# Where the first group's square and the weights' rests are computed, in a fused attention and two-stage MLP kernel on one core

## The chip, the core and the metric

The kernel runs on one core of one Trainium2 chip. The metric is the device time of one execution in microseconds (us), and smaller is better. The engines are called PE (matrix multiply), DVE (vector), ACT (scalar, activation), POOL (GpSimd) and SP (which issues most DMAs). PEld is the loading of weights into PE. Each engine takes its own instructions in order, and engines wait for one another by semaphores.

## The reference

Three stages are chained. The change lies in the second, and in what prepares its weights.

```python
# 1. attention with a window of 32, half of the heads dilated by 4 (4 x 8 heads x 576 positions x 64)
attn = softmax(where(mask, q @ k.T / 8, -1e9)); x = attn @ v          # -> x: 2304 x 512
# 2. a dense two-layer block, 512 -> 2048 -> 512
h = x @ w_in
r = maximum(h, 0)
g = s * (r * r) + b                                                   # s, b: one number each
y = g @ w_out
# 3. each token goes to the best of 8 experts (512 -> 1024 -> 512), times its gate
out[token] = gate * (maximum(y @ w1[e], 0) @ w2[e])
```

The weights of stage 2 (`w_in`, `w_out`) arrive as 64-bit floats, so they are converted on the chip.

## The kernel before, in words

**Numbers in two parts.** PE multiplies a rounded 32-bit format (F32R). Each operand X is kept as a rounded part and a rest, X = hi + lo, and `mm3` (L271) issues three matmuls: hi·hi, hi·lo, lo·hi. So whatever enters a matmul is first rounded by one engine (a copy to F32R on ACT), and then its rest is taken as a subtraction.

**Stage 2.** The 2304 tokens go in six groups `g` of 384. For each group the hidden width of 2048 is walked in 16 chunks `fc` of 128. `gemm1(g, fc)` (L277) does 12 matmuls into `ph`, then four elementwise steps on 128 x 384: ACT takes `r` = relu (L284), DVE makes `r` = s·r·r (L285), ACT rounds `gh` = r + b (L288), DVE takes the rest `gl` = (r + b) − gh (L289). `gemm2(g, fc)` (L293) multiplies gh, gl by the chunk's `woh`, `wol` into three accumulators `py`, two chunks behind `gemm1`. The tiles r, gh, gl have two buffers each.

**Weights.** `weight_prep(which, fc)` (L246) converts one tile of 128 x 512. `which` is 0 for `w_in` (tiles `wih`, `wil`) and 1 for `w_out` (tiles `woh`, `wol`). The steps are: SP loads `raw` (L252 or L255, three buffers), DVE shifts (`cv`, L260, two buffers), ACT scales (`ce`, L262, one buffer), POOL adds the two (L263), DVE merges sign and exponent (L264), ACT rounds to `wih` or `woh` (L267), and the rest is taken (L269): on DVE for `w_in`, on POOL for `w_out`. There are 32 such tiles: eight are begun while the first eight units of attention run (`attn_first`, L183), and the others are called two for each turn of the main loop (L356 to L385) during the first group.

**Attention** runs in units. `attn_b` computes scores on PE (`pS`, L128) and the softmax: L134, L137 on DVE, exp L139 on ACT, L141, L142 and the scaling of `prob` (L145) on DVE. `attn_c` transposes `prob` on PE (`pT`, L153) and copies it (`sT`, L158, ACT); `attn_d` multiplies by v on PE (`po`, L172). The units of the next group are put between the chunks of this one at fixed slots. Before the main loop PE also transposes the experts' embedding (`pemb`, L347), whose load `embn` (L344) takes one of the three `raw` buffers.

**Order.** In the main loop PE's instructions stand in the order in which the program is written. The order on DVE, ACT, POOL and SP is made by a planner that simulates the program with costs of its own and starts what it takes to be ready. The experts' stage follows after the last group.

Of the kernel before, what the change touches and what calls it, by code (L numbers as in the profile page):

```python
# [7 lines left out]
F32 = mybir.dt.float32  # L8
# [3 lines left out]
AF = mybir.ActivationFunctionType  # L12
ALU = mybir.AluOpType
# [15 lines left out]
PERIOD, START = 6, 2  # L29
LA = 2  # L30
EARLY = 10
SPLIT = EARLY - LA

P = 128
# [13 lines left out]
class Kern:  # L48
# [180 lines left out]
    def weights_setup(self, left, right):  # L229
        self.xhi, self.xlo, self.wih, self.wil, self.woh, self.wol = [[] for _ in range(6)]  # L230
        for f in range(16):
            pool = right if f < SPLIT else left
            self.woh.append(pool.tile([P, DM], F32R, name=f"woh{f}"))
            self.wol.append(pool.tile([P, DM], F32R, name=f"wol{f}"))
        for f in range(16):
            pool = right if f < EARLY else left
            self.wih.append(pool.tile([P, 4, P], F32R, name=f"wih{f}"))
# [8 lines left out]
    def weight_prep(self, which, fc):  # L246
        nc, sp = self.nc, self.spool
        u = f"{which}{fc}"
        raw = sp.tile([P, 512, 2], I32, tag="raw", name=f"raw{u}", bufs=3)
        fs = slice(P * fc, P * fc + P)  # L250
        if which == 0:
            nc.sync.dma_start(out=raw.rearrange("p f w -> p (f w)"), in_=self.w_in.bitcast(I32)[fs])  # L252
            hi, lo = (x[fc].rearrange("p k f -> p (k f)") for x in (self.wih, self.wil))
        else:
            nc.sync.dma_start(out=raw.rearrange("p f w -> p (f w)"), in_=self.w_out.bitcast(I32)[fs])  # L255
            hi, lo = self.woh[fc], self.wol[fc]
        w0, w1 = raw[:, :, 0], raw[:, :, 1]
        t = sp.tile([P, 512], I32, tag="cv", name=f"cv{u}", bufs=2)
        e = sp.tile([P, 512], I32, tag="ce", name=f"ce{u}", bufs=1)
        nc.vector.tensor_scalar(out=t, in0=w1, scalar1=3, scalar2=0x3FFFFFFF,  # L260
                                op0=ALU.logical_shift_left, op1=ALU.bitwise_and)
        nc.scalar.mul(e, w0.bitcast(U32), 2.0 ** -29)  # L262
        nc.gpsimd.tensor_tensor(out=t, in0=t, in1=e, op=ALU.add)  # L263
        nc.vector.scalar_tensor_tensor(out=t, in0=w1, scalar=-0x40000000, in1=t,  # L264
                                       op0=ALU.bitwise_and, op1=ALU.bitwise_or)
        tf = t.bitcast(F32)
        nc.scalar.copy(hi, tf)  # L267
        eng = nc.vector if which == 0 else nc.gpsimd
        eng.tensor_sub(lo, tf, hi.bitcast(F32))  # L269

    def mm3(self, out, ah, al, bh, bl, first, last):  # L271
        nc = self.nc
# [4 lines left out]
    def gemm1(self, g, fc):  # L277
        nc, mp, pm = self.nc, self.mpool, self.psM
        xh, xl = self.xhi[g % 2], self.xlo[g % 2]
        ph = pm.tile([P, 512], F32, tag="ph", name=f"ph{g}_{fc}", bufs=2)  # L280
        for kc in range(4):
            self.mm3(ph[:, :G], self.wih[fc][:, kc], self.wil[fc][:, kc], xh[:, kc], xl[:, kc], kc == 0, kc == 3)
        r = mp.tile([P, G], F32, tag="r", name=f"r{g}_{fc}")
        nc.scalar.activation(r, ph[:, :G], AF.Relu)  # L284
        nc.vector.scalar_tensor_tensor(out=r, in0=r, scalar=self.sb[:, 0:1], in1=r, op0=ALU.mult, op1=ALU.mult)  # L285
        gh = mp.tile([P, G], F32R, tag="gh", name=f"gh{g}_{fc}")
        gl = mp.tile([P, G], F32R, tag="gl", name=f"gl{g}_{fc}")
        nc.scalar.activation(gh, r, AF.Identity, bias=self.sb[:, 1:2])  # L288
        nc.vector.scalar_tensor_tensor(out=gl, in0=r, scalar=self.sb[:, 1:2], in1=gh.bitcast(F32),  # L289
                                       op0=ALU.add, op1=ALU.subtract)  # L290
        self.gt[g, fc] = gh, gl

    def gemm2(self, g, fc):  # L293
# [27 lines left out]
    def phase1(self, first_pools, late, late_pools):  # L321
# [28 lines left out]
        with tc.tile_pool(name="mp", bufs=2, reuse_waits="tile") as self.mpool, tc.tile_pool(name="psM", bufs=1, space=PSUM, reuse_waits="tile") as self.psM:  # L350
# [5 lines left out]
            for i in range(NG * 16 + LA):  # L356
# [4 lines left out]
                if i == (33 - self.wi) // 2:  # L361
                    sp_cm.__exit__(None, None, None)
                    ep_cm = tc.tile_pool(name="ep", bufs=1, side="right", reuse_waits="tile")
                    self.emb_setup(ep_cm.__enter__())
                if i == 16 * (NG - 1) + EARLY:
                    assert not steps and not self.bg
# [5 lines left out]
                    early = [(0, self.experts_early1), (2, self.experts_early2), (6, self.experts_early3)]  # L372
                if early and i == 16 * (NG - 1) + EARLY + early[0][0]:
                    early.pop(0)[1]()
# [719 lines left out]
```

## Time and profile before

| | |
|---|---|
| time, median of 3 runs | 799.92 us (799.87 to 800.5) |
| time of the profiled execution | 798.41 us |
| its span (first to last instruction) | 796.6 us |
| PE busy | 756.1 us (95%) |
| DVE busy | 571.1 us (72%) |
| ACT busy | 388.1 us (49%) |
| POOL busy | 124.4 us (16%) |
| mean granted TensorE clock | 0.99 of full speed |

The times of the views count from the start of the span. A row of a view names the line, the engine, the operation, "out<-in" by the program's names, the shape and the count. "Idle before" is the time in which the engine did nothing just ahead of such an instruction, and the arrow names who released it.

### The profile page before, as it was taken

Reading aid. Unit: us, or ns where it says so; the run is one execution under the profiler, and the core shown is the slowest. Engines: PE = TensorE matmul, PEld = TensorE weight load, DVE = VectorE, ACT = ScalarE, POOL = GpSimd, SP = SyncE. Lnnn points to the kernel's source line nnn. Section 1 sums busy time; section 2 is a strip of 40 time slices with the busy share of each in tenths; the row PEclk is TensorE's granted clock in tenths of the full one; section 3 lists DMA queues with packets and bytes.
Section 4 is the critical chain, followed back from the end, with each engine's and each line's share of the span. In section 5 each row is a group of like instructions: output and inputs, shape, how many; then the busy total and the mean of one; then the engine's idle time right before and its main releaser. Section 6 shows DMA issues by size and latency. Waiting matters only on the chain. (4 is left out here: it accounts for less than half of the span.)

```text
span 796.6 us, 14252 instructions
## 1 busy us (share of the span) xinstructions
PE 756.1 (95%) x5154; PEld 668.3 (84%) x5154; DVE 571.1 (72%) x1362; ACT 388.1 (49%) x909; POOL 124.4 (16%) x107
## 2 busy tenths in 40 slices
PE   5677888999999999999999999999999999999996
PEld 4467777888988898889888999889988989898895
DVE  5888999786657765766576749857856868777671
ACT  5655665544354435443544442552525656546550
POOL 2554565000000000000000000020420222211010
PEclk9998999999999999999999999999999999999999
DMA  7655553412011201120110010520326129797710
GB/s 260 200 179 172 177 177 96 168 46 83 18 62 46 81 20 62 46 80 22 62 46 18 1 40 1 203 84 19 92 72 206 58 89 302 236 319 239 252 65 25
DMA packets 33373, 88.05 MB, mean 111 GB/s; under 512 B 4294, under 2 KB 4294, under 8 KB 33168
## 3 DMA queue, kind: packets, MB, share of 16 engines
q1 hardware_dynamic: 29936, 76.84, 29.2%
q0 software_dynamic: 3360, 10.23, 3.9%
q8 instruction: 43, 0.70, 0.4%
q14 instruction: 34, 0.28, 0.1%
HBM read 94.39 MB, written 10.22 MB: 131 GB/s over the span
## 5 line engine op out<-in xcount | busy, mean ns | idle before, releaser
L798 DVE TENSOR_TENSOR wl<-raw,wh 128x1024 fp32r<-128x1024 f32 x96 | 113.6, 1221 | 29.4 <-ACT wh L797 29.4
L273 PE MATMUL ph<-xhi,wih 128*128 128x384 f32 x384 | 130.6, 340 | 0.1
L275 PE MATMUL ph<-xhi,wil 128*128 128x384 f32 x384 | 130.1, 339 | 0.5 <-DVE wil L269 0.5
L274 PE MATMUL ph<-xlo,wih 128*128 128x384 f32 x384 | 129.8, 338 | 0.0
L273 PE MATMUL py<-woh,gh 128*128 128x512 f32 x288 | 119.5, 415 | 0.1
L275 PE MATMUL py<-woh,gl 128*128 128x512 f32 x288 | 115.2, 400 | 1.5 <-DVE gl L289 1.5
L274 PE MATMUL py<-wol,gh 128*128 128x512 f32 x288 | 114.9, 399 | 0.0
L289 DVE SCALAR_TENSOR_TENSOR gl<-r,sb,gh 128x384 fp32r<-128x384 f32 x96 | 66.7, 695 | 50.2 <-ACT gh L288 47.9
L288 ACT ACTIVATE gh<-r,sb 128x384 fp32r<-128x384 f32 x96 | 58.9, 614 | 82.7 <-PE py L274 65.2
L797 ACT CAST wh<-raw 128x1024 fp32r<-128x1024 f32 x96 | 96.1, 1054 | 5.6 <-DMA raw<-in_moe_w 5.5
L284 ACT ACTIVATE r<-ph 128x384 f32<-128x384 f32 x96 | 46.8, 488 | 98.8 <-PE ph L275 97.4
L285 DVE SCALAR_TENSOR_TENSOR r<-r,sb 128x384 f32<-128x384 f32 x96 | 63.2, 658 | 35.6 <-ACT r L284 35.3
L507 DVE CUSTOM_DVE_ANT_0 junk<-ysb,enb 128x512 bf16<-128x512 f32 x120 | 82.5, 687 | 0.9
L273 PEld LDWEIGHTS ph<-xhi,wih 128*128 128x128 f32 x384 | 72.8, 190 | 4.3 <-ACT r L284 0.3
L274 PEld LDWEIGHTS ph<-xlo,wih 128*128 128x128 f32 x384 | 72.6, 189 | 4.0
L139 ACT ACTIVATE prob<-prob,st 128x80 f32<-128x80 f32 (+3 forms) x168 | 58.5, 350 | 31.0 <-DVE st L137 31.0
L275 PEld LDWEIGHTS ph<-xhi,wil 128*128 128x128 f32 x384 | 72.5, 189 | 0.9 <-DVE wil L269 0.9
L273 PE MATMUL ph<-xh,wh 128*128 128x256 f32 x256 | 72.7, 284 | 0.0
L274 PE MATMUL ph<-xl,wh 128*128 128x256 f32 x256 | 72.6, 284 | 0.0
L275 PE MATMUL ph<-xh,wl 128*128 128x256 f32 x256 | 72.3, 283 | 0.0
L275 PEld LDWEIGHTS py<-woh,gl 128*128 128x128 f32 x288 | 55.1, 191 | 15.0 <-DVE gl L289 2.4
L273 PE MATMUL po<-wh,hh 128*128 128x512 f32 x168 | 66.8, 398 | 0.0
(252 smaller groups left out, 1376.2 us busy)
## 6 DMA issues: line engine op xcount, KB each, us to landing
raw<-in_moe_w SPq DMA_DIRECT2D x96, 512.0 KB
raw<-in_moe_w_in SPq DMA_DIRECT2D x16, 512.0 KB
raw<-in_moe_w_out SPq DMA_DIRECT2D x16, 512.0 KB
qkd<-in_qkd SPq DMA_DIRECT2D x24, 288.0 KB
qkp<-in_qkp SPq DMA_DIRECT2D x12, 416.0 KB
ydram<-ysb SPq DMA_DIRECT2D x18, 256.0 KB
vd<-in_vd SPq DMA_DIRECT2D x24, 160.0 KB
vp<-in_vp SPq DMA_DIRECT2D x12, 288.0 KB
```

What stands on the lines that cost most here:

```text
L139: nc.scalar.activation(prb[:, t, :w], prb[:, t, :w], AF.Exp, scale=-1.0, bias=st[:, t:t + 1], accum_out=st[:, 4 + t:5 + t])
L273: nc.tensor.matmul(out, lhsT=ah, rhs=bh, start=first, stop=False)
L274: nc.tensor.matmul(out, lhsT=ah, rhs=bl, start=False, stop=False)
L275: nc.tensor.matmul(out, lhsT=al, rhs=bh, start=False, stop=last)
L284: nc.scalar.activation(r, ph[:, :G], AF.Relu)
L285: nc.vector.scalar_tensor_tensor(out=r, in0=r, scalar=self.sb[:, 0:1], in1=r, op0=ALU.mult, op1=ALU.mult)
L288: nc.scalar.activation(gh, r, AF.Identity, bias=self.sb[:, 1:2])
L289: nc.vector.scalar_tensor_tensor(out=gl, in0=r, scalar=self.sb[:, 1:2], in1=gh.bitcast(F32), op0=ALU.add, op1=ALU.subtract)
L507: ins = nc.vector.tensor_tensor_reduce(out=self.junk, in0=y, in1=self.enb[:, e], scale=1.0, scalar=0.0, op0=ALU.mult, op1=ALU.add, accum_o ...
L797: nc.scalar.copy(h, r)
L798: nc.vector.tensor_sub(l, r, h.bitcast(F32))
```

## The change

In group 0 (`g < SQUARES`, with SQUARES = 1), ACT squares r in place, then rounds gh from s·r + b with s and b as operands of one activation. DVE makes s·r + b in place with one two-operation instruction, and takes gl as a plain subtraction. The groups 1 to 5 keep their four steps. In `weight_prep` the rest of `w_out` is taken on DVE as that of `w_in` is, so that POOL keeps only the additions of L263.

```diff
+SQUARES = 1
@@ weight_prep
         nc.scalar.copy(hi, tf)
-        eng = nc.vector if which == 0 else nc.gpsimd
-        eng.tensor_sub(lo, tf, hi.bitcast(F32))
+        nc.vector.tensor_sub(lo, tf, hi.bitcast(F32))
@@ gemm1
         nc.scalar.activation(r, ph[:, :G], AF.Relu)
-        nc.vector.scalar_tensor_tensor(out=r, in0=r, scalar=self.sb[:, 0:1], in1=r, op0=ALU.mult, op1=ALU.mult)
         gh = mp.tile([P, G], F32R, tag="gh", name=f"gh{g}_{fc}")
         gl = mp.tile([P, G], F32R, tag="gl", name=f"gl{g}_{fc}")
-        nc.scalar.activation(gh, r, AF.Identity, bias=self.sb[:, 1:2])
-        nc.vector.scalar_tensor_tensor(out=gl, in0=r, scalar=self.sb[:, 1:2], in1=gh.bitcast(F32),
-                                       op0=ALU.add, op1=ALU.subtract)
+        if g < SQUARES:
+            nc.scalar.activation(r, r, AF.Square)
+            nc.scalar.activation(gh, r, AF.Identity, scale=self.sb[:, 0:1], bias=self.sb[:, 1:2])
+            nc.vector.tensor_scalar(out=r, in0=r, scalar1=self.sb[:, 0:1], scalar2=self.sb[:, 1:2], op0=ALU.mult, op1=ALU.add)
+            nc.vector.tensor_sub(gl, r, gh.bitcast(F32))
+        else:
+            nc.vector.scalar_tensor_tensor(out=r, in0=r, scalar=self.sb[:, 0:1], in1=r, op0=ALU.mult, op1=ALU.mult)
+            nc.scalar.activation(gh, r, AF.Identity, bias=self.sb[:, 1:2])
+            nc.vector.scalar_tensor_tensor(out=gl, in0=r, scalar=self.sb[:, 1:2], in1=gh.bitcast(F32),
+                                           op0=ALU.add, op1=ALU.subtract)
```

## Rows read from the trace of the kernel before

**Rows 1.** Three stretches: length, busy us of each engine (count), PEclk, DMA.

```profile
40.00:139.30 99.30, 82.34 (x567) 71.12 (x568) 90.95 (x145) 60.32 (x151) 56.63 (x38) 0.93 0.50 161
139.30:460.00 320.70, 320.52 (x2356) 284.99 (x2355) 217.79 (x674) 144.54 (x444) 0.00 (x0) 1.00 0.16 53
460.00:796.60 336.60, 329.01 (x1980) 293.61 (x1979) 234.05 (x466) 158.35 (x225) 51.67 (x42) 1.00 0.41 136
```

**Rows 2.** PE's waits, 40 to 139.3 us: total us, times, longest.

```profile
PE pT L153 <- DVE prob L145: 12.8, 6, 4.2
PE pT L153 <- ACT wih L267: 2.6, 1, 2.6
PE ph L275 <- DVE wil L269: 0.5, 1, 0.5
```

**Rows 3.** DVE's groups, 40 to 140 us: busy us, mean ns, idle before.

```profile
L264 DVE SCALAR_TENSOR_TENSOR cv<-raw,cv 128x512 int32<-128x512 int32 x26 | 26.6, 1023 | 3.0 <-POOL cv L263 3.0
L289 DVE SCALAR_TENSOR_TENSOR gl<-r,sb,gh 128x384 fp32r<-128x384 f32 x15 | 16.7, 1115 | 1.8 <-ACT gh L288 1.8
L285 DVE SCALAR_TENSOR_TENSOR r<-r,sb 128x384 f32<-128x384 f32 x16 | 13.8, 861 | 0.0
L269 DVE TENSOR_TENSOR wil<-cv,wih 128x512 fp32r<-128x512 f32 x13 | 13.2, 1015 | 1.2 <-ACT wih L267 1.1
L260 DVE TENSOR_SCALAR cv<-raw 128x512 int32<-128x512 int32 x25 | 12.9, 514 | 2.5 <-DMA raw<-in_moe_w_in 2.4
```

**Rows 4.** DVE in order of time: start, duration; POOL is idle until 85.51.

```profile
83.22 0.60 DVE L285 SCALAR_TENSOR_TENSOR r<-r,sb 128x384 f32<-128x384 f32 x1
83.74 0.68 DVE L269 TENSOR_TENSOR wil<-cv,wih 128x512 fp32r<-128x512 f32 x1
84.35 0.68 DVE L264 SCALAR_TENSOR_TENSOR cv<-raw,cv 128x512 int32<-128x512 int32 x1
84.95 0.41 DVE L260 TENSOR_SCALAR cv<-raw 128x512 int32<-128x512 int32 x1
```

**Rows 5.** POOL's groups, 0 to 140 us.

```profile
L263 POOL TENSOR_TENSOR cv<-cv,ce 128x512 int32<-128x512 int32 x32 | 47.2, 1474 | 58.6 <-ACT ce L262 21.8 <-DVE cv L260 21.3 <-ACT prob L139 3.3
L269 POOL TENSOR_TENSOR wol<-cv,woh 128x512 fp32r<-128x512 f32 x16 | 23.1, 1446 | 6.9 <-ACT woh L267 6.9
```

**Rows 6.** POOL in order of time: first and last of 13 rests after 40 us.

```profile
46.07 1.28 POOL L269 TENSOR_TENSOR wol<-cv,woh 128x512 fp32r<-128x512 f32 x1
...
137.96 1.29 POOL L269 TENSOR_TENSOR wol<-cv,woh 128x512 fp32r<-128x512 f32 x1 [1.88 <-ACT woh L267]
```

**Rows 7.** DVE in order of time, beside the two rests of Rows 6.

```profile
46.16 1.75 DVE L264 SCALAR_TENSOR_TENSOR cv<-raw,cv 128x512 int32<-128x512 int32 x1 [1.18 <-POOL cv L263]
...
138.50 1.16 DVE L289 SCALAR_TENSOR_TENSOR gl<-r,sb,gh 128x384 fp32r<-128x384 f32 x1 [0.74 <-ACT gh L288]
```

**Rows 8.** ACT's groups, 40 to 139.3 us.

```profile
L288 ACT ACTIVATE gh<-r,sb 128x384 fp32r<-128x384 f32 x15 | 9.2, 611 | 6.5 <-DVE r L285 3.5 <-PE py L274 2.8 <-PE pT L153 0.3
...
L284 ACT ACTIVATE r<-ph 128x384 f32<-128x384 f32 x16 | 7.7, 479 | 1.3 <-PE ph L275 1.2
```

**Rows 9.** ACT's groups over the span: a Square, and all table loads.

```profile
L504 ACT ACTIVATE junk<-ysb 128x512 bf16<-128x512 f32 x15 | 9.4, 629 | 0.2
...
L139 ACT ACT_TABLE_LOAD x1 | 1.3, 1283 | 0.8 <-PEq L1078 0.8
```

**Rows 10.** DVE in order of time, in the first stretch.

```profile
30.58 1.48 DVE L260 TENSOR_SCALAR cv<-raw 128x512 int32<-128x512 int32 x1 [0.89 <-POOL wol L269]
```

**Rows 11.** PE's longest wait just ahead of the main loop.

```profile
PE pemb L347 <- DMA embn<-in_moe_expert_emb: 2.7, 1, 2.7
```

**Rows 12.** The instructions of `py` in two stretches (PE, PEld, ACT), then PEclk.

```profile
64.20:67.70 3.50, 3.41 (x9) 2.62 (x9) 0.00 (x0) 0.59 0.45 154
72.00:74.20 2.20, 2.17 (x9) 1.62 (x9) 0.00 (x0) 1.00 0.84 177
```

## Prediction

> **What bounds the kernel now.** I read the busy times of all engines stretch by stretch first, since the share over the span mixes stages. From 139.3 to 460 us PE is busy 320.52 of 320.70 us at full clock, and after that 329.01 of 336.60 [rows 1]. Groups 1 to 5, which the change leaves as they are, can't become faster through DVE, ACT or POOL: PE runs through them in its written order. Whatever the change gains or loses comes before 139.3 us, and shifts all that follows.
>
> In the 99.3 us from 40 to 139.3 us PE is busy 82.34 us, so 17.0 us are open, and DVE is the fullest engine with 90.95 us; ACT has 60.32, POOL 56.63 [rows 1]. The second view is PE's waits: 12.8 us of the 17.0 are transposes that wait for DVE's `prob`. A further 2.6 us are put down to ACT's `wih`, but a transpose doesn't read that; it stands at the same place, ahead of a unit's first transpose, so I count it with `prob`. A rest on DVE costs 0.5 us [rows 2]. So PE waits for DVE, and it waits for attention, not for the weights: the softmax of the next group stands in DVE's queue behind the weights and the four steps of gemm1.
>
> The third view is what fills DVE. Where POOL is idle, L264 and L269 take 0.68 us, L285 0.60, L260 0.41 [rows 4]; L289 has the form of L285. Their means in the stretch are 1.023, 1.015, 0.861, 0.514 and, for L289, 1.115 us [rows 3]. The surplus is 26·0.34 + 13·0.33 + 16·0.26 + 25·0.10 + 15·0.51 = 8.9 + 4.4 + 4.2 + 2.6 + 7.7 = 27.8 us. It comes in lumps of about a microsecond that end when a POOL instruction ends: the L264 at 46.16 took 1.75 us, and the POOL rest that had started at 46.07 ended at 47.35; the L289 at 138.50 took 1.16, against a POOL rest from 137.96 to 139.25 [rows 6, 7]. So a DVE instruction of these kinds that meets a running POOL instruction stands until that ends. POOL ran 38 instructions here [rows 1]: 27.8/38 = 0.73 us of DVE for each.
>
> **The change part by part.** All sums are against the profiled execution (798.41 us, span 796.6, 1.8 us around it); the median of the runs is 799.92, 1.5 us above it, and I take gains off the median.
>
> *POOL's rests go.* 13 of the 38 lie in this stretch. By the mean they cost DVE 13·0.73 = 9.5 us. Taken one by one, in order of time from the pair at 46.07 to the pair at 137.96, 12 of the 13 have a DVE instruction that stands behind them, by 1.07 us at the first (1.75 − 0.68), 0.56 at the last and 1.11 at most, in sum 11.7 us. I take 10.6, the middle.
>
> *They come back on DVE.* 13 subtractions of the form of `wil`. From the start of one to the start of the next it is 83.74 to 84.35, 0.61 us [rows 4]: +7.9 us.
>
> *s·r·r becomes s·r+b.* The L285 costs 0.52 us from start to start [rows 4]. The new instruction has one tensor input. The nearest row is L260, also with two operations on one tensor: 0.41 us for 512 elements, 0.33 without the 0.08 that neighbours overlap [rows 4]; for 384 three quarters, 0.25. The other bound is that it costs what L285 did, with no gain. It is of L260's kind, so I take 0.26: 15 times 0.26 saved, −3.9 us (bounds −4.1 and 0). The surplus of 4.2 us that L285 had from POOL's additions is not credited, since another instruction will stand there instead. L289 becomes a plain subtraction of two tensors; L264 and L269 both take 0.68, so it costs the same.
>
> *ACT.* The square: L284 takes 0.479 on 384 elements, a Square on 512 takes 0.629 [rows 8, 9], so 0.48 to 0.63, say 0.49; 16 of them are 7.8 us. `gh` gets a second operand per partition. It takes 0.611 with one and L284 0.479 with none [rows 8], so it becomes 0.61 to 0.74: up to 2.1 us more. Both lie in ACT's 39 idle microseconds of this stretch [rows 1], and in return `gh` no longer waits for DVE's L285 (3.5 us) [rows 8]. I cost them at nothing. If that cover were gone, the softmax's exponentials would stand behind squares: for the eight units of this stretch at most one square each, 4 us. A table load costs 1.283 us, but there is one in the whole span although Square and Exp alternate in groups 1 to 5 [rows 9], so none is added.
>
> The Trainium skill (ScalarE: Activation LUTs, What ACT_TABLE_LOAD costs) says that each per-partition operand adds about 93 ns to an activation. The trace has 0.13 us between none and one, with a PSUM source on the one side, and no row with two. By the page `gh` would grow by 16·0.093 = 1.5 us in all, an estimate inside the bound above.
>
> *Sum in the stretch:* −10.6 + 7.9 − 3.9 = −6.6 us of DVE. A microsecond of DVE is worth one of PE as long as PE still waits for `prob`, and 6.6 is well under 17.0.
>
> *Before 40 us.* Three POOL rests lie here. One is plainly on the path: the L260 at 30.58 waited 0.89 us for it, because `cv` has two buffers, and then took 1.48 instead of 0.41 because the addition which that rest had delayed was running [rows 10]. That is 1.96 us of DVE for one rest of 0.61. Behind it stand the scaling of `prob`, two merges (L264) and with them the buffer for `embn`, for which PE waits 2.7 us before the main loop [rows 11]. I take 1.3 us, between 0 and those 2.7. Later loads of `raw` wait for the same merges and move with them.
>
> *Clock.* Nine `py` matmuls take 3.41 us in 64.2 to 67.7, at a granted clock of 0.59 (largely the lower level, 1.2 GHz), and 2.17 at full clock, 2.4 GHz [rows 12]; ahead of the first stretch PE had stood still for `prob`. Two more such stretches follow long waits (83.8 and 122.7 us), 3.9 us together. Shorter waits give part of that back. I take 1.3, between 0 and 3.9.
>
> *Total* −6.6 − 1.3 − 1.3 = −9.2, so 799.92 − 9.2 = 790.7 us. What is late next: PE still waits for `prob`, for some 10 us instead of 17.
>
> **The rivals.**
>
> *All waits go* (PE the bound from 40 us on). Against it: DVE would have to hold some 84 us of work in 82 us. For it: the planner may put the softmax earlier once gemm1's chain needs one DVE step less. 17.0 + 3.9 + 1.3 = 22.2 less: 777.7 us.
>
> *The lock waits refill.* 25 additions stay, and DVE is full, so each may find an instruction at the door. At 1.05 us each, about the usual single wait, they cost 26.3 us instead of 27.8 in all. Then DVE has −1.5 + 7.9 − 3.9 = +2.5; with the additions at 0.9 us each (22.5) it has −5.3 + 7.9 − 3.9 = −1.3. With the 1.3 us of the first stretch that is 801.1 to 797.3, middle 799.2. For it: there is one more contending DVE instruction for each chunk, eight for seven. Against it: additions cost 0.73 on average with DVE as full as it is. The Trainium skill bears on this (SBUF — State Buffer, Who interferes with whom): a DVE instruction with two SBUF inputs, or in a 2-port mode as tensor_scalar has it, and a GpSimd instruction exclude each other, and the order of issue, not the shape, decides who blocks. By it the added subtractions and s·r+b contend as much as what they replace, which is what makes this rival possible; the trace agrees in that L264, L269 and L260 all show the surplus.
>
> *DVE stands for the casts* (slower). On POOL the rest of `w_out` waited 6.9 us in all for ACT's cast [rows 5], with nothing behind it but additions. On DVE the whole queue stands behind it. If the planner puts each rest right behind its merge, DVE waits a cast (0.62 us) and a handoff, some 0.72 us, 13 times, 9.4 us: −6.6 + 9.4 = +2.8, so 802.7. It decides from 0.5 us for each rest on. Against it: `wil` has the same place, and DVE waited 1.1 us for its casts in 13 rests [rows 3].
>
> *It does nothing that can be measured:* weights set the pace. PE waited 0.5 us for a `wil` [rows 2], near the end; if PE comes earlier, the weights' chain of six steps may hold it instead. Against it: additions start sooner without rests ahead of them on POOL. 799 to 801.
>
> **How the numbers follow.** A measurement of this kernel tells about 0.2%, 1.6 us, from no change. Forecast (784 to 796) 0.60, all waits go 0.16, refill 0.09, no effect 0.06, casts 0.09. The likeliest is the forecast: 790.7. From 780 to 799.5 leaves out about 0.08 below (half of the first rival) and some 0.12 to 0.15 above (casts, parts of refill and no effect). Faster by over 0.2% is the forecast, the first rival and about half of the refill, 0.80; within 0.2% the rest of the refill and no effect, 0.11; slower 0.09.
>
> **What would show it.** Right: POOL with 32 additions only, none of them much longer than now; the DVE surplus between 40 and 131 us at 17 to 20 us; s·r+b near 0.33 us; PE waits for `prob` of 6 to 10 us; the last weight done some 8 us earlier; groups 1 to 5 as long as now. Wrong: L264 and L145 with means above today's (refill), DVE idle behind ACT's `woh` (casts), table loads beside the squares, or a DVE order in which the softmax comes later than now.

## The result, and the profile after

The changed kernel takes 792.49 us, the median of four runs (790.65 to 793.61), against 800.0 for the kernel before: a ratio of 0.9903 [0.9883, 0.9923], or 7.8 us less. The prediction was 790.7 in a range of 780 to 799.5. The profiled execution took 792.93 us with a span of 791.1, so its span is 5.5 us shorter than that of before (which lay 1.5 us under its median, this one 0.4 above). I divide the spans at the first matmul of `gemm1` and at the first copy of `y` by ACT, which stands at the end of group 0, and call what lies between them the main stretch. The kernel before, by stretches (length, busy us and count of PE, PEld, DVE, ACT, POOL, then PEclk, DMA share, GB/s):

```profile
0.00:40.13 40.13, 24.38 (x256) 18.64 (x256) 28.44 (x80) 24.84 (x89) 16.09 (x27) 1.00 0.70 229
40.13:149.16 109.03, 92.08 (x632) 79.69 (x632) 94.78 (x154) 62.53 (x155) 56.63 (x38) 0.94 0.50 166
```

The kernel after: the same two stretches, then two that answer to the two later ones of [rows 1] (the first begins at 131.90, just behind this kernel's last weight), then two pairs of five microseconds out of the main stretch.

```profile
0.00:40.46 40.46, 24.16 (x257) 18.60 (x257) 30.30 (x85) 25.74 (x90) 13.59 (x25) 1.00 0.71 228
40.46:142.47 102.01, 93.77 (x631) 81.70 (x632) 89.79 (x165) 70.07 (x171) 36.26 (x25) 0.95 0.54 177
...
131.90:460.00 328.10, 328.05 (x2396) 292.32 (x2395) 219.31 (x676) 147.36 (x449) 0.00 (x0) 1.00 0.16 52
460.00:791.10 331.10, 323.37 (x1944) 288.57 (x1942) 231.99 (x462) 156.63 (x222) 51.72 (x42) 0.99 0.41 138
...
55.00:60.00 5.00, 1.78 (x11) 1.22 (x10) 4.86 (x10) 4.20 (x9) 2.13 (x2) 1.00 0.43 138
60.00:65.00 5.00, 5.00 (x19) 4.31 (x17) 4.01 (x8) 2.03 (x4) 2.50 (x2) 0.66 0.40 122
...
90.00:95.00 5.00, 3.36 (x17) 2.51 (x16) 5.00 (x16) 3.73 (x9) 2.32 (x2) 0.93 0.34 115
95.00:100.00 5.00, 5.00 (x20) 4.24 (x20) 4.86 (x8) 3.29 (x7) 2.31 (x2) 0.73 0.61 170
```

Read them as an account. Up to the main stretch, 40.13 us became 40.46: +0.3. The main stretch went from 109.03 to 102.01: −7.0. Everything behind it took 647.4 us before and 648.6 after; 1.2 us is within what executions differ by there: from the last copy of `y` to the end alone, the profiles of this study took from 260.0 to 262.5 us. Inside the main stretch, the time in which PE is not busy fell from 109.03 − 92.08 = 16.95 us to 102.01 − 93.77 = 8.24 us, by 8.7. PE's busy time did not fall; it is 1.7 us longer. The last pairs show what held it up: after 3.2 us without work in 55 to 60 us, the granted clock is 0.66 in the next five, partly at the lower level of 1.2 GHz. The same happens at 95 us (0.73), and from 125 to 135 us (0.84 and 0.82). Over the main stretch the granted clock is 0.95, where it was 0.94 before.

PE's waits after, 40.4 to 131.9 us (total us, times, longest), which answer to [rows 2]:

```profile
PE ph L275 <- DVE wil L269: 2.2, 3, 1.0
PE pT L154 <- ACT r L288: 1.9, 1, 1.9
PE pT L154 <- DVE prob L146: 1.3, 1, 1.3
PE pT L154 <- ACT gh L289: 1.2, 1, 1.2
PE ph L273 <- ACT wih L268: 1.2, 1, 1.2
PE ph L273 <- DVE xlo L182: 1.1, 1, 1.1
```

The transposes `pT` read neither `r` nor `gh`. Those waits stand ahead of a unit's first transpose, and I count them with `prob`, as before. That makes 4.4 us for the softmax, where [rows 2] had 15.4 counted in the same way. The weights, `wil` and `wih`, now cost 3.4 us where they cost 0.5. They do so from 114 us on. The wait for `xlo` ends where the main stretch begins; the others make up its 8.2 us of open time, with 0.4 us for `sT`, not shown here.

DVE's groups after, 40 to 131 us by form (busy us, mean ns, idle before), which answer to [rows 3]. L265 is the merge, L290 the new s·r+b, L269 the two rests, L261 the shift, L291 the new subtraction for `gl`:

```profile
L265 DVE SCALAR_TENSOR_TENSOR cv<-raw,cv 128x512 int32<-128x512 int32 x25 | 18.0, 722 | 0.0
L290 DVE TENSOR_SCALAR r<-r,sb 128x384 f32<-128x384 f32 x15 | 14.6, 972 | 1.0 <-ACT gh L289 1.0
L269 DVE TENSOR_TENSOR wil<-cv,wih 128x512 fp32r<-128x512 f32 x13 | 13.5, 1040 | 1.8 <-ACT wih L268 1.8
L261 DVE TENSOR_SCALAR cv<-raw 128x512 int32<-128x512 int32 x24 | 10.8, 450 | 1.2 <-DMA raw<-in_moe_w_in 0.8 <-DMA raw<-in_moe_w_out 0.2
L269 DVE TENSOR_TENSOR wol<-cv,woh 128x512 fp32r<-128x512 f32 x13 | 9.9, 759 | 0.2 <-ACT woh L268 0.2
L291 DVE TENSOR_TENSOR gl<-r,gh 128x384 fp32r<-128x384 f32 x15 | 9.0, 598 | 0.4
```

DVE in order of time (start, us): the new instruction where POOL does not run, and, in the first stretch, a scaling of `prob` that stood behind an addition of POOL:

```profile
48.74 0.47 DVE L290 TENSOR_SCALAR r<-r,sb 128x384 f32<-128x384 f32 x1
49.13 0.44 DVE L135 SCALAR_TENSOR_TENSOR prob<-pS,mask 128x288 f32<-128x288 f32 x1
...
32.82 0.68 DVE L265 SCALAR_TENSOR_TENSOR cv<-raw,cv 128x512 int32<-128x512 int32 x1
33.42 1.56 DVE L146 TENSOR_TENSOR prob<-prob,st 128x320 f32<-128x320 f32 x1
```

ACT's groups after, 40 to 131 us, which answer to [rows 8]; L288 is the square:

```profile
L289 ACT ACTIVATE gh<-r,sb 128x384 fp32r<-128x384 f32 x15 | 10.6, 705 | 2.6 <-PE py L274 2.4
...
L288 ACT ACTIVATE r<-r 128x384 f32<-128x384 f32 x15 | 7.9, 524 | 0.1
```

POOL's largest group after, 0 to 150 us, which answers to [rows 5]: 32 additions, no longer than before (1474 ns there), and no rests.

```profile
L264 POOL TENSOR_TENSOR cv<-cv,ce 128x512 int32<-128x512 int32 x32 | 46.9, 1466 | 77.0 <-DVE cv L261 29.9 <-ACT ce L263 23.9 <-DVE st L142 10.0
```

### The profile page after: what moved, and what is told of

Its sections match the earlier page's. It is cut to its first block, busy times and chain, and to the rows that moved or that the text cites. A ratio compares the mean times of both kernels' runs of the same rounds, so it can differ in the third digit from the quotient of the medians.

```text
span 791.1 us, 14275 instructions
## 1 busy us (share of the span) xinstructions
PE 758.8 (96%) x5154; PEld 671.9 (85%) x5154; DVE 566.8 (72%) x1378; ACT 396.5 (50%) x925; POOL 101.6 (13%) x91
## 5 line engine op out<-in xcount | busy, mean ns | idle before, releaser
L275 PE MATMUL ph<-xhi,wil 128*128 128x384 f32 x384 | 131.9, 343 | 2.2 <-DVE wil L269 2.2
L294 ACT ACTIVATE gh<-r,sb 128x384 fp32r<-128x384 f32 x80 | 49.1, 614 | 75.6 <-PE py L274 61.8
L295 DVE SCALAR_TENSOR_TENSOR gl<-r,sb,gh 128x384 fp32r<-128x384 f32 x80 | 49.3, 616 | 48.9 <-ACT gh L294 46.5
L293 DVE SCALAR_TENSOR_TENSOR r<-r,sb 128x384 f32<-128x384 f32 x80 | 49.3, 617 | 36.1 <-ACT r L284 35.8
```

Source lines behind the costliest of these rows:

```text
L275: nc.tensor.matmul(out, lhsT=al, rhs=bh, start=False, stop=last)
```

## The experiments

Times are medians; each ratio is against the kernel before, run on the same chip (799.5 to 800.4 us). Differences in us to that kernel are taken from the ratios, and differences between two experiments from those.

**1. The rests alone.** ACT's square and the new chunk steps are taken out again.

```diff
-SQUARES = 1
+SQUARES = 0
```

> The rests of w_out go to DVE; gemm1 of group 0 keeps its four steps. Theory A (the two parts add up as shares of DVE's queue): -10.6 + 7.9 = -2.7 us of DVE, with some clock given back about -3.5: 795.5 to 798, that is some 40% of what the whole change gains. Rival B (the gain is gemm1's chain, which no longer passes through DVE's queue between relu and gh): 799 to 801. Rival C (the gain is POOL's lock alone): 792 to 793.5. DVE's surplus over undisturbed durations falls from 27.8 us to 16 to 20 in all three.

Measured: 795.31 us, ratio 0.9948 [0.9935, 0.9961], −4.2 us. Moving the rests alone makes the kernel faster, by a little more than was expected. The rival that DVE would stand for the casts had it slower.

**2. The square alone.** The rests of `w_out` go back to POOL.

```diff
-        nc.vector.tensor_sub(lo, tf, hi.bitcast(F32))
+        eng = nc.vector if which == 0 else nc.gpsimd
+        eng.tensor_sub(lo, tf, hi.bitcast(F32))
```

> ACT squares and DVE makes s*r+b in group 0; the rests of w_out stay on POOL. Theory A: DVE saves 0.18 to 0.26 us for each of 16 chunks, 2.9 to 4.2 us: 795 to 797.5. Rival B (gemm1's chain): 791.5 to 794. Rival C (POOL's lock alone): 799 to 801. DVE's surplus from POOL stays at 26 to 29 us.

Measured: 797.07 us, ratio 0.9976 [0.9962, 0.9990], −1.9 us [−3.0, −0.8], less than the 2.9 to 4.2 us of DVE that were expected. The two parts have 6.1 us together, the whole change 7.8 [6.2, 9.4]; to the width of the intervals they add up.

**3. More buffers for the weights.** If the chain of the weights were held by its buffers, three `cv` and two `ce` would let it run ahead.

```diff
-        t = sp.tile([P, 512], I32, tag="cv", name=f"cv{u}", bufs=2)
-        e = sp.tile([P, 512], I32, tag="ce", name=f"ce{u}", bufs=1)
+        t = sp.tile([P, 512], I32, tag="cv", name=f"cv{u}", bufs=3)
+        e = sp.tile([P, 512], I32, tag="ce", name=f"ce{u}", bufs=2)
```

> The changed kernel with three cv buffers for two and two ce buffers for one; nothing else. In its trace PE waited near the end of the first group for wil and wih, 3.4 us in four waits. If the weights' chain is held by its buffers, POOL's next addition no longer waits for ACT's ce to come free and the chain ends earlier: 788.5 to 791. If it is held by DVE's queue, which is as full as before, buffers change nothing: 791.5 to 793.5.

Measured: 801.31 us, ratio 1.0024 [1.0012, 1.0037]: some 9 us slower than the changed kernel, a miss. PE's waits in this kernel, 40 to 150 us:

```profile
PE pT L154 <- DVE prob L146: 6.2, 3, 3.1
PE pT L154 <- ACT woh L268: 3.8, 1, 3.8
PE ph L273 <- DVE xlo L182: 3.0, 1, 3.0
PE py L275 <- DVE gl L291: 2.2, 1, 2.2
```

No wait for a weight is left, and the waits for the softmax and for `xlo` are long again: the planner put the conversion, which it now took to be ready, ahead of the softmax in DVE's queue. All 96 steps of the weights on DVE stand ahead of the last scaling of `prob` in this stretch, against 78 in the changed kernel. The granted clock of the execution was 0.973, against 0.989 of the changed kernel. Buffers and order changed together here, so that the order alone costs this much is argued from these waits. If so, it is worth as much as the whole change, and every edit that alters what the planner takes to be ready alters the order too.

**4. No additions on POOL.** The two parts of a word are joined on DVE by a bitwise or. What it leaves out is the carry out of the low three bits; the rest of the computation stays. POOL then has nothing to do in this stretch.

```diff
-        nc.gpsimd.tensor_tensor(out=t, in0=t, in1=e, op=ALU.add)
+        nc.vector.tensor_tensor(out=t, in0=t, in1=e, op=ALU.bitwise_or)
```

> The changed kernel with the joining of the two words (L264) on DVE, as a bitwise or in place of the addition; a carry out of the low three bits is left out, so weights differ by some 1e-6. POOL does nothing before the experts' stage. Theory A (each POOL instruction costs DVE some 0.65 us): DVE gains 25 x 0.61 = 15.3 us of work and loses all of its surplus of 16 us, the chain loses a handoff to POOL: 789 to 793, the surplus 0 to 1 us. Rival D (the surplus is DVE's own, from two large inputs, and not POOL's): DVE has 15 us more, 800 to 806, with the surplus as it was.

Measured: 781.21 us, ratio 0.9768 [0.9756, 0.9781], −18.6 us, well below what was expected. DVE's groups in this kernel, 40 to 140 us by form (L264 is the or):

```profile
L264 DVE TENSOR_TENSOR cv<-cv,ce 128x512 int32<-128x512 int32 x24 | 16.5, 687 | 0.7 <-ACT ce L263 0.3
L265 DVE SCALAR_TENSOR_TENSOR cv<-raw,cv 128x512 int32<-128x512 int32 x24 | 16.4, 685 | 0.0
...
L269 DVE TENSOR_TENSOR wol<-cv,woh 128x512 fp32r<-128x512 f32 x13 | 8.9, 684 | 0.0
...
L290 DVE TENSOR_SCALAR r<-r,sb 128x384 f32<-128x384 f32 x16 | 7.6, 474 | 3.3 <-ACT gh L289 3.3
```

Its main stretch:

```profile
37.55:131.80 94.25, 89.07 (x632) 77.53 (x632) 84.45 (x194) 68.48 (x171) 0.00 (x0) 1.00 0.57 192
```

The means are those of undisturbed instructions: L290 fell from 972 to 474 ns. The rival, that the surplus is DVE's own, had it at 800 to 806 us. DVE took over 25 joins, 17.2 us busy, and is nevertheless 5.3 us less busy than in the changed kernel (84.45 against 89.79). The main stretch is 7.8 us shorter than there (94.25 against 102.01), of which 3.1 are open time (5.18 against 8.24) and 4.7 are PE's own busy time (89.07 against 93.77): the clock is 1.00 throughout where the changed kernel has three stretches below it. Another 2.9 us come before it, where the first matmul of `gemm1` moves from 40.46 to 37.55.

**5. No rests of `w_out` at all.** From the kernel before, the rest is left out and the second matmul reads the rounded part in its place, so this term of the product is not the reference's. It prices the rests on POOL.

```diff
-        eng = nc.vector if which == 0 else nc.gpsimd
-        eng.tensor_sub(lo, tf, hi.bitcast(F32))
+        if which == 0:
+            nc.vector.tensor_sub(lo, tf, hi.bitcast(F32))
@@ gemm2
-            self.mm3(self.py[i], gh[:, ts], gl[:, ts], self.woh[fc], self.wol[fc], fc == 0, fc == 15)
+            self.mm3(self.py[i], gh[:, ts], gl[:, ts], self.woh[fc], self.woh[fc], fc == 0, fc == 15)
```

> The kernel before, with the rests of w_out left out altogether: the matmuls read woh in place of wol, so y is not the reference's. Theory A: POOL's 13 rests cost 10.6 us of DVE by the lock, and with the clock some 11: 787 to 790; with the run that moved the rests to DVE (795.3) that makes 5.5 to 8 us the price of the rests on DVE. Rival (a rest on POOL is free as long as nobody waits for its result): 797.5 to 800.

Measured: 793.08 us (789.99 to 796.24), ratio 0.9917 [0.9888, 0.9946], −6.6 us [−9.0, −4.3]: by the times the rests on POOL cost less than was expected. Against experiment 1 the same rests on DVE cost 2.5 us (0.9948 − 0.9917, of 800 us), with some 2 to 3 us of uncertainty from the spread of this kernel. In its trace group 0 ends at 139.38 us instead of 149.16, which is 9.8 us earlier; 1.7 us are lost again right behind it, where PE waits for ACT's copy of `y`. DVE's shift in this kernel, 40 to 131 us:

```profile
L260 DVE TENSOR_SCALAR cv<-raw 128x512 int32<-128x512 int32 x24 | 14.1, 587 | 5.5 <-DMA raw<-in_moe_w_in 2.5 <-DMA raw<-in_moe_w_out 2.4 <-ACT prob L139 0.4
```

Once the rests are gone, DVE waits 5.5 us ahead of the shift, mostly for loads of the weights, where [rows 3] has 2.5.

**6. One more activation for each chunk.** `gh` is written twice, to see whether ACT's time is covered.

```diff
             nc.scalar.activation(gh, r, AF.Identity, scale=self.sb[:, 0:1], bias=self.sb[:, 1:2])
+            nc.scalar.activation(gh, r, AF.Identity, scale=self.sb[:, 0:1], bias=self.sb[:, 1:2])
```

> The changed kernel with gh written twice in group 0, one more activation of some 0.7 us on ACT for each chunk, 16 in all. Theory (ACT's part is covered by its idle time): 791.5 to 794.5. Rival (ACT stands on the path: what the square costs there hides part of the gain): 16 x 0.6 = 9.6 us, 798 to 803.

Measured: 793.0 us, ratio 0.9913 [0.9896, 0.9929]. Sixteen activations more cost 0.5 us by the medians and 0.8 by the ratios, which the runs can't tell from nothing. In time ACT is covered. In the trace the main stretch is as long as in the changed kernel (102.03 us), but PE stands open for 11.40 us in it instead of 8.24 and is busy for 90.63 instead of 93.77, at a clock of 0.98 instead of 0.95. So no run shows that the work on ACT costs no wait at all.

**7. The square in all groups.**

```diff
-SQUARES = 1
+SQUARES = 6
```

> The changed kernel with the square on ACT in all six groups instead of the first. If groups 1 to 5 are bound by PE alone, their DVE and ACT work is covered either way: 791 to 794, as the changed kernel (792.5). Rival (DVE's saved time counts there too, 5 x 2 us): 781 to 787; or ACT becomes late for the softmax there: 796 to 802.

Measured: 790.04 us, ratio 0.9878 [0.9863, 0.9894], which overlaps the changed kernel's. Five more groups with the cheaper step bring nothing that these times can tell. In the traces there is a little: from the end of group 0 to the last copy of `y` it takes 384.95 us instead of 386.60, and 0.9 us of that is open time of PE in group 5. So groups 1 to 5 are PE's but for a microsecond or two.

**8. The or on DVE, without the square.** To price the square where POOL doesn't disturb; as in experiment 4 the carry out of the low three bits is left out, here and in the next three.

```diff
 # against experiment 4
-SQUARES = 1
+SQUARES = 0
```

> As the run with the words joined on DVE (781.2, a carry out of the low three bits left out), but gemm1 of group 0 keeps its four steps. If the square's part is worth what DVE saves by it, 0.18 us for each of 16 chunks, whatever else stands in DVE's queue: 783 to 785. If its gain came from lock waits that L285 no longer takes, it is gone without POOL: 780.5 to 782.5.

Measured: 783.06 us, ratio 0.9786 [0.9765, 0.9807]: 1.4 us above experiment 4 by the ratios, 1.9 by the medians, with an uncertainty of some 2 us. That agrees with the 1.9 us of experiment 2, but it is not clear of nothing either. In the traces the main stretch is 1.7 us longer than in experiment 4 (95.93 against 94.25), 0.4 of it open time of PE and 1.3 its busy time at a clock of 0.93. So whether the square is worth as much without POOL as with it stays open.

**9. Work on POOL that nobody reads.** To experiment 4 a subtraction on POOL is added behind every rest, from the rounded weight into a scratch tile. No engine waits for it.

```diff
 # against experiment 4
         nc.vector.tensor_sub(lo, tf, hi.bitcast(F32))
+        sc = sp.tile([P, 512], F32R, tag="sc", name=f"sc{u}", bufs=1)
+        nc.gpsimd.tensor_sub(sc, hi.bitcast(F32), hi.bitcast(F32))
```

> As the run with the words joined on DVE (781.2), and POOL subtracts each rounded weight tile from itself into a scratch tile that nobody reads: 32 POOL instructions of the size of a rest, for which no engine waits. Theory A (a running POOL instruction stops DVE's next one): 25 x 0.65 = 16 us of DVE after 40 us, of which 7 to 13 reach PE: 788 to 794, and L264, L265, L269 have means of 0.8 to 1.1 us again. Rival E (that run was faster since the weights' chain no longer passes through POOL): 780 to 783.

Measured: 802.09 us, ratio 1.0022 [1.0011, 1.0032]: 20.3 us (by the ratios) above experiment 4, and much more than was expected. DVE's 270 instructions of the first stage and group 0 stand in the same order as in experiment 4, ACT's up to the first copy of `y` too, and no engine waits for the new ones. So this is the cost of POOL's instructions and not of another order: 20.3/32 = 0.63 us of the kernel for each. DVE's groups in this kernel, 40 to 140 us by form:

```profile
L264 DVE TENSOR_TENSOR cv<-cv,ce 128x512 int32<-128x512 int32 x25 | 19.4, 775 | 0.4
L269 DVE TENSOR_TENSOR wil<-cv,wih 128x512 fp32r<-128x512 f32 x13 | 12.3, 946 | 0.1
...
L292 DVE TENSOR_SCALAR r<-r,sb 128x384 f32<-128x384 f32 x15 | 10.4, 694 | 1.5 <-ACT gh L291 1.5
L293 DVE TENSOR_TENSOR gl<-r,gh 128x384 fp32r<-128x384 f32 x14 | 10.2, 728 | 0.0
```

Its main stretch:

```profile
40.25:151.83 111.58, 94.13 (x631) 80.00 (x632) 103.34 (x195) 69.75 (x172) 39.34 (x26) 0.95 0.50 162
```

Against the stretch of experiment 4, DVE is 103.34 − 84.45 = 18.9 us busier with the same instructions, 0.73 us for each of the 26 subtractions there, and the stretch is 17.3 us longer. Of that 12.3 us are open time of PE (17.45 against 5.18) and 5.1 us are PE's busy time at a clock of 0.95. The other 2.7 us come before it.

**10. Work on POOL that reads nothing.** The same, with a memset in place of the subtraction; one column, copied by ACT, ties it to the same place.

```diff
 # against experiment 4
         nc.vector.tensor_sub(lo, tf, hi.bitcast(F32))
+        sc = sp.tile([P, 1024], F32, tag="sc", name=f"sc{u}", bufs=1)
+        nc.scalar.copy(sc[:, 0:1], hi[:, 0:1].bitcast(F32))
+        nc.gpsimd.memset(sc, 0.0)
```

> As the run with idle POOL subtractions (802.1), but POOL fills a scratch tile of 128x1024 instead, an instruction that reads nothing, tied to the same cast by a copy of one column on ACT. If what stops DVE is that both read SBUF through one port, two-input instructions (L264, L265, L269, gl) keep their undisturbed 0.55 to 0.69 us and only one-input ones (L261, s*r+b) are stopped: 783 to 788. If DVE stops whenever POOL runs at all: as in that run, 0.6 us and more for each of 32 instructions, 798 to 804.

Measured: 781.55 us, ratio 0.9778 [0.9764, 0.9791], as experiment 4 within its interval, and below the 783 to 788 that were expected if reading is what counts. POOL's group in this kernel, 40 to 150 us:

```profile
L272 POOL MEMSET sc<- 128x1024 f32 x25 | 24.1, 965 | 58.8 <-ACT sc L271 58.8
```

DVE's groups in it, 40 to 140 us by form:

```profile
L265 DVE SCALAR_TENSOR_TENSOR cv<-raw,cv 128x512 int32<-128x512 int32 x25 | 17.2, 687 | 0.0
...
L261 DVE TENSOR_SCALAR cv<-raw 128x512 int32<-128x512 int32 x24 | 11.4, 475 | 1.5 <-DMA raw<-in_moe_w_in 1.5
L293 DVE TENSOR_SCALAR r<-r,sb 128x384 f32<-128x384 f32 x16 | 8.9, 556 | 2.9 <-ACT gh L292 2.9
```

POOL is busy 24.1 us here, and the instructions of DVE with two tensor inputs are as short as in experiment 4 (687 ns against 685). Only those with one input lengthen a little: L261 from 423 to 475 ns, s·r+b from 474 to 556. In the main stretch DVE is 2.1 us busier than in experiment 4 (86.53 against 84.45), where experiment 9 had 18.9. So it is not that POOL is busy, but that it reads. The Trainium skill (SBUF — State Buffer, Who interferes with whom) says that a DVE instruction with two SBUF inputs contends with a GpSimd instruction that reads SBUF and not with one that only writes it, and that a tensor_scalar in a 2-port mode contends as well; these runs agree with the first, and with the second in that the one-input steps lengthen beside the memset. In which mode those steps ran, no run shows.

**11. The root of s in the square.** ACT squares r·√s, so that DVE has one step for each chunk instead of two (√s is computed once at the start).

```diff
 # against experiment 4
-            nc.scalar.activation(r, r, AF.Square)
-            nc.scalar.activation(gh, r, AF.Identity, scale=self.sb[:, 0:1], bias=self.sb[:, 1:2])
-            nc.vector.tensor_scalar(out=r, in0=r, scalar1=self.sb[:, 0:1], scalar2=self.sb[:, 1:2], op0=ALU.mult, op1=ALU.add)
-            nc.vector.tensor_sub(gl, r, gh.bitcast(F32))
+            nc.scalar.activation(r, r, AF.Square, scale=self.rs)
+            nc.scalar.activation(gh, r, AF.Identity, bias=self.sb[:, 1:2])
+            nc.vector.scalar_tensor_tensor(out=gl, in0=r, scalar=self.sb[:, 1:2], in1=gh.bitcast(F32),
+                                           op0=ALU.add, op1=ALU.subtract)
@@ at the start
+            y = self.rsqrt(self.lpool, self.sb[:, 0:1], 1, "rs")
+            self.rs = self.lpool.tile([P, 1], F32, name="rs")
+            self.nc.vector.tensor_mul(self.rs, y, self.sb[:, 0:1])
```

> As the run with the words joined on DVE (781.2), and ACT squares r with the root of s as its scale, so that s*r*r comes out at once; DVE then takes the rest in the one instruction it had before (0.53 us from start to start in place of 0.39 + 0.47), and gh has one operand per partition. DVE has 16 x 0.33 = 5.3 us less, and 2 us more at the very start, where it is idle. If DVE still sets the pace: 777.5 to 780; if the remaining time is PE's own and the loads': 780.5 to 782.

Measured: 781.6 us (778.72 to 783.99), ratio 0.9771 [0.9746, 0.9796]. The main stretch of its profile is 91.16 us with PE busy for 88.09 and DVE for 79.88, against 94.25, 89.07 and 84.45 in experiment 4, but the time is the same within the intervals: the stretch starts 1.3 us later (38.86 against 37.55), and what lies behind it took 1.8 us more (649.9 against 648.1). With PE open for 3.1 us there, little is left for DVE to give. No version that ran is clearly faster than experiment 4.

## Why the prediction came out, point by point

The direction, the place and the main mechanism were right, and the total was 1.8 us off. That it is so near is in part luck. PE's open time fell by 8.7 us where 6.6 were forecast, and that made up for part of two terms that went the other way: the start (+0.3 for −1.3) and PE's busy time (+1.7 for −1.3). The stretches also account for only the 5.5 us between the two profiled spans; the rest of the 7.8 lies in which executions were profiled. Main-stretch totals of the kernels that bear on it, from the stretches of their profiles (us):

| | start | length | PE busy | open |
|---|---|---|---|---|
| before | 40.13 | 109.03 | 92.08 | 16.95 |
| after | 40.46 | 102.01 | 93.77 | 8.24 |
| 1: rests alone | 40.45 | 106.21 | 93.21 | 13.00 |
| 2: square alone | 40.22 | 106.24 | 91.62 | 14.62 |
| 4: or on DVE | 37.55 | 94.25 | 89.07 | 5.18 |
| 5: no rests of `w_out` | 38.03 | 101.35 | 91.38 | 9.97 |
| 6: `gh` twice | 40.19 | 102.03 | 90.63 | 11.40 |
| 8: 4 without the square | 38.20 | 95.93 | 90.36 | 5.57 |
| 9: 4 with reading work on POOL | 40.25 | 111.58 | 94.13 | 17.45 |
| 10: 4 with writing work on POOL | 38.05 | 95.19 | 89.87 | 5.32 |

**PE waits for the softmax behind DVE; groups 1 to 5 are PE's.** Right. The open time fell by 8.7 us, `prob`'s share from 15.4 to 4.4. From 131.9 to 460 us PE is busy 328.05 of 328.10 us, and experiment 7 bounds what a cheaper step there can bring: nothing that the times can tell, 1.7 us in the trace.

**A POOL instruction that runs stops a DVE instruction, 0.73 us for each.** Right for instructions that read, and shown by experiments 9 and 10: 0.73 us of DVE and 0.63 us of the kernel for each reading instruction, with DVE's order unchanged, and nothing that can be told for each writing one. By the same five groups as the prediction used, the surplus after is 25·0.04 + 15·0.50 + 13·0.36 + 13·0.08 + 24·0.04 + 15·0.05 = 15.9 us, taking 0.684 us for L265 and L269, 0.474 for L290, 0.41 for L261 and 0.55 for L291; a little under the 17 to 20 of the forecast. For each of the 25 additions that is 0.64 us.

**The rests: −10.6 on POOL, +7.9 on DVE, net −2.7.** The net came out better than forecast, at −4.2 [−5.2, −3.1] (experiment 1). The two terms by themselves came out smaller as time of the kernel, 6.6 us [4.3, 9.0] (experiment 5) and about 2.5 (experiment 5 against 1). As time of DVE they did not. The stretch from the first matmul of `gemm1` to DVE's last rest, before, in experiment 5 and in experiment 1, one execution each:

```profile
40.13:136.62 96.49, 79.59 (x552) 68.52 (x551) 88.89 (x143) 58.62 (x148) 55.34 (x37) 0.93 0.51 165
38.03:123.82 85.79, 75.82 (x537) 65.66 (x537) 77.36 (x138) 56.32 (x145) 34.08 (x25) 0.94 0.57 188
40.45:136.33 95.88, 82.88 (x563) 72.42 (x564) 87.80 (x155) 59.15 (x150) 36.65 (x25) 0.93 0.50 166
```

DVE's busy time falls by 11.5 us without the rests and rises by 10.4 with the rests on DVE. Group 0 ended 9.8 us earlier and then 7.3 us later in these profiles (149.16, 139.38, 146.66). So the terms were not too large as DVE's time; the step that failed is that a microsecond of DVE is worth one of PE. Where the rest of it went stays open. DVE waits longer for loads without the rests (5.5 us ahead of the shift), but all its idle time in this stretch grew by only 0.8 us (7.6 to 8.4), and the planner's order differs between these kernels too. In the changed kernel as a whole the exchange went the other way: in the main stretch DVE is 5.0 us less busy (94.78 to 89.79), and PE's open time fell by 8.7.

**s·r·r becomes s·r+b: −3.9.** The size was off. What was mis-sized is the duration taken from the shift: 0.33 us was forecast, and undisturbed it takes 0.47, 0.39 from start to start. Its two scalars come from a tile where the shift has constants; whether that is the reason no run isolates. The subtraction for `gl`, forecast at no difference, is 0.05 us shorter than the step that it replaces (0.55 against 0.60). Together DVE saves 0.18 us for each chunk, 2.7 us for 15. The kernel saves 1.9 [0.8, 3.0] in experiment 2; the 1.4 of experiment 8 is not clear of nothing. Of DVE's groups this one has the largest surplus: its mean is 972 ns, 0.50 above its own, 7.5 of the 15.9 us of surplus.

**ACT at nothing.** Right in time, by experiment 6. The square took 0.524 us (0.48 to 0.63 forecast), `gh` 0.705. The second operand cost 94 ns, and no table load was added. The Trainium skill (ScalarE: Activation LUTs, What ACT_TABLE_LOAD costs) gives about 93 ns for each per-partition operand, and the row agrees.

**Before 40 us: −1.3.** This failed; the first matmul of `gemm1` came 0.3 us later. The chain that was argued did get shorter (PE's wait for the experts' embedding fell from 2.7 to 0.7 us), but the planner put another merge ahead of the last unit's scaling of `prob`, which then ran into an addition and took 1.56 us. PE's wait for that `prob` rose from 2.7 to 4.4 us, and it waited 1.1 us for `xlo` behind it.

**Clock: −1.3.** This failed as well. The prediction read three stretches at a lower clock, and took part of them away because the waits ahead of them would shorten. They shortened, and three such stretches are still there: PE's busy time is 1.7 us longer, not shorter. In experiment 4 the clock is 1.00 throughout the main stretch and PE's busy time 4.7 us less. So the term was real, but the changed kernel has gained nothing of it. It is also part of why experiment 4 won more than was expected (4.7 us), and experiment 9 lost more (5.1 us): there a loss on DVE came twice, as a wait and then as slower matmuls.

**The rivals.** *DVE stands for the casts*: refuted; DVE waited 0.2 us for `woh` in 13 rests, and experiment 1 is faster. *The lock waits refill*: refuted for this change, since the surplus fell from 27.8 to 15.9 us, though the new instruction does meet the additions as that rival feared. *All waits go*: 8.2 us stay open. *No effect, since weights set the pace*: not yet, but this is what comes next. `wil` and `wih` cost 3.4 us at the end of group 0, where the forecast saw only `prob`, at 6 to 10 us; `prob` has 4.4. The last rest ended at 130.8 us, 8.5 earlier than before (8 forecast).

**What stays open** is how much of each difference between two kernels with different orders is the order itself. Experiment 3 suggests that it can be 9 us. Only experiments 9 and 10 against 4, where the order is the same or nearly so, are free of it.

## What to carry to other kernels

When a helper engine's instructions lengthen those of the engine that is full, price them by what they add there, not by the helper's own busy share: here 32 reading instructions that nothing waited for cost 20 us, and moving POOL's work onto the *fuller* DVE won both times (experiments 1 and 4). Price a step by a row with the same kinds of operands (scalars from a tile or constants, one tensor or two), and price a gain on a waiting engine together with what the wait does to PE's clock afterwards. Where a planner sets the order, test a cause with an edit that leaves the order as it is.

## What the runs showed of the hardware that was not expected

- A POOL instruction that reads cost 0.63 us of the kernel, and those that only write cost nothing that can be told, although POOL was busy with them for 24 us (experiments 9 and 10).
- POOL can be the one that starves. A subtraction of which the median is 1.2 us took 3.72 in experiment 9, while DVE went through five of its own without a gap and at their undisturbed lengths; only then did an s·r+b take 1.20 in place of 0.47. POOL, in order of time:

```profile
102.47 3.72 POOL L271 TENSOR_TENSOR sc<-woh 128x512 fp32r<-128x512 f32 x1 [2.53 <-ACT woh L268]
```

and DVE beside it:

```profile
102.60 0.55 DVE L293 TENSOR_TENSOR gl<-r,gh 128x384 fp32r<-128x384 f32 x1
103.07 0.68 DVE L269 TENSOR_TENSOR wol<-cv,woh 128x512 fp32r<-128x512 f32 x1
103.67 0.68 DVE L264 TENSOR_TENSOR cv<-cv,ce 128x512 int32<-128x512 int32 x1
...
105.21 1.20 DVE L292 TENSOR_SCALAR r<-r,sb 128x384 f32<-128x384 f32 x1
```

- A DVE instruction with one tensor and two scalars out of a tile took 0.47 us on 128 x 384, more than the 0.41 of one with constants on 128 x 512 [rows 4]. The operations and the number formats differ between the two as well.
